# The loads of raw w_out move from the queue of SP to the queue of GpSimd

## The chip, the cores and the metric

One core of one Trainium2 chip runs the whole program. The metric is device time in microseconds (us): the median of several executions. Engines are named as in the profile: PE (TensorE), PEld (its weight load), DVE (VectorE), ACT (ScalarE), POOL (GpSimd), SP (SyncE, which here only begins transfers).

## The reference

```python
batch, n_heads, seq, head_dim = (4, 12, 448, 64)
scores = scale * np.matmul(q, k.transpose(0, 1, 3, 2))
scores = np.einsum('bhij,hg->bgij', scores, w_pre)
scores = scores - np.max(scores, axis=-1, keepdims=True)
attn = np.exp(scores)
attn = attn / (np.sum(attn, axis=-1, keepdims=True) + 1e-09)
attn = np.einsum('bhij,hg->bgij', attn, w_post)
x = np.matmul(attn, v)        # heads side by side: (1792, 768)
h = x @ w_in                  # (768, 2048)
g = h * np.clip(h + 3.0, 0.0, 6.0) / 6.0
out = g @ w_out               # (2048, 768)
```

An attention whose heads are mixed before and after the softmax, and a two-layer network on its output. w_in and w_out arrive as float64.

## The kernel before, in words

The work is cut into operations, and a planner (class `Plan`) sets the order of each engine's instructions before the program is built. Every operation names its engine, an assumed duration, what it reads and writes, and a priority. `Plan.schedule` goes forward in assumed time: each engine takes the ready operation of lowest priority number, and transfers pass through an assumed bandwidth kept per queue in `bw`. What comes out is a fixed order per engine. On the chip each engine and each queue keeps that order: an instruction that waits holds all that stand behind it.

**Attention** runs in steps s of 10 query rows (`step`, 45 per batch, R = 2 halves each in most). For 60 query rows, `scores` makes the products of queries and keys (L448), ACT copies them out of PSUM (`s`, L473), and small transfers on SP spread them by head into a tile `T_one` or `T_two` (L480, one instruction per head, 12 for each m, drawn `T_one<-s`). Then PE mixes the heads (L533), DVE takes the row maximum (`nb`, L541), ACT the exponential (`e`, L542), POOL scales the sum (`sm`, L544), DVE inverts it (`r`, L545), POOL multiplies (L551), ACT rounds to 16 bits (`eh`, L553), POOL forms the remainder (`el`, L554), PE mixes again (L570), and after some steps PE multiplies by the values (L607).

**The first layer** (`moe1`, L828) is independent work for PE that the planner puts between the steps; its results go to DRAM (`gd<-g`, L846).

**The weights.** `w_out_decode` is called 24 times, for n from 0 to 23. Each call loads 512 KB of raw float64 words (`wo<-in_w_out`, begun at L789 through `bulk`, L352 to L354, which uses SP) into one of the two places of the ring `stw`; ACT and DVE make float32 of it (L676, L679, L683, L687, L691); DVE forms sums and differences (L781); `w_store` sends the results to DRAM (`wsd<-WF`, L778). A load can begin when DVE has read the raw words of two calls earlier (L691). The decoded tiles go round in four places of `WF`, so a sum also waits for the store that still reads its place. All 24 loads fall into the attention, between 226 and 529 us.

**The second layer** (L1109) multiplies by the combinations of w_out in seven products per batch. It runs from about 560 us to the end.

Of the kernel before, what the change touches and what calls it, by code (L numbers as in the profile page):

```python
# [27 lines left out]
P = 128  # L28
# [35 lines left out]
Z_AT = 30  # L64
LAT_0, ACT_T = 1.0, 1
S_BUFS, LAT_T, LAT_B = 3, 2.0, 3.0


class Op:
# [50 lines left out]
class Plan:  # L120
# [64 lines left out]
    def schedule(self, prio, stay):  # L185

        free, wait, ready, out = {}, {}, {}, []
        bw, mode, then = {"SP": 0.0, "ACT": 0.0}, None, None
        recent = collections.deque([(0.0, 0.5, 0.5)], 60)
        for o, n in zip(self.ops, self.counts):  # L190
            o.n, o.ready, o.end = n, 0.0, None
# [22 lines left out]
        def avail(o):  # L214
            t = o.ready
            for p in {b.pool for b in o.takes}:
                x = p.ready(sum(b.pool is p for b in o.takes), self.HOP)
                if x is None:
                    return None
                t = max(t, x)  # L220
            return t

        while True:
            best = None
            for e in free:
                if e == "PE":
                    at = [(avail(x[2]), x) for x in ready[e]]
                    at = [(x, z) for x, z in at if x is not None]
                    if not at:
                        continue  # L230
                    t = max(free[e], min(at)[0])
                elif ready[e]:
                    t = free[e]
                elif wait[e]:
                    t = max(free[e], wait[e][0][0])
# [6 lines left out]
            t, e = best  # L242
            if e == "PE":
                at = [(avail(x[2]), x) for x in ready[e]]
                at = [x for z, x in at if z is not None and z <= t + 1e-9]
                x = min(at)
                x = min([z for z in at if z[2] is then] or [z for z in at if z[2].mode == mode and z[0] < x[0] + stay] or [x])
                then = x[2].then
# [15 lines left out]
            if e == "PE":  # L264
                n, fn, z = fill
# [5 lines left out]
            if e == "PE":  # L271
                o.end += self.SWITCH * (mode not in (None, o.mode))
                mode = o.mode
            free[e] = o.end
            if o.bytes:
                x, d, other = max(bw[e], t + 1.1), o.bytes / self.DMA_RATE, "ACT" if e == "SP" else "SP"
# [28 lines left out]
def body(ctx: ExitStack, tc: tile.TileContext, q4, kT, vj, wpre0, wpost0, ident0, w_in, w_out, outT):  # L305
    nc = tc.nc
    PE, ACT, DVE, POOL, SP = nc.tensor, nc.scalar, nc.vector, nc.gpsimd, nc.sync
# [14 lines left out]
    plan = Plan()  # L322
# [3 lines left out]
    def buf(pool, shape, dt, tag, name, bufs=1, ring=True):  # L326

        g = rings.setdefault((id(pool), tag), Ring(bufs)) if ring else None
        return Buf(lambda: pool.tile(shape, dt, tag=tag, name=name, bufs=bufs), g)
# [16 lines left out]
    def dma(nbytes, fn, r, w, prio, after=()):  # L346
        return plan.op("SP", 0.5, fn, r, w, prio, after, nbytes)

    def dmas(nbytes, out, src, w, prio, after=()):
        return plan.op("SP", 0.5, lambda: SP.dma_start(out(), src), [], w, prio, after, nbytes)  # L350

    def bulk(nbytes, out, src, w, prio, after=()):  # L352
        q = BULK
        return plan.op(q, 0.5 if q == "SP" else 0.4, lambda: (SP if q == "SP" else ACT).dma_start(out(), src), [], w, prio, after, nbytes, lat=LAT_B)  # L354
# [397 lines left out]
    def w_out_scale(z, n, room, prio):  # L752
        m, am1, t, p, r = (const([P, 1], F32, f"wo_{x}_{z}") for x in ("m", "am", "t", "p", "r"))
        dve(0.2, lambda: DVE.tensor_reduce(m(), wo_st()[:, :n], axis=AX.X, op=ALU.max), [(wo_st, k) for k in range(n)], [m], prio)
        top = across(m, f"wo{z}", prio + 0.1)

        def f():
            pow64(top, am1, t, p, r)
            if room > 1:
                DVE.tensor_scalar(p(), p(), float(room), None, op0=ALU.mult)  # L760
                DVE.tensor_scalar(r(), r(), 1.0 / room, None, op0=ALU.mult)

        dve(1.3, f, [top], [am1, t, p, r], prio + 0.2)
        wo_p[z], wo_r[z] = p, r
# [3 lines left out]
    def w_place():  # L768
        if not wr_ring.all:
            z = Buf(None)  # L770
            z.uses = [u for x in wf_ring.all[-3:] for u in x.uses]
            wr_ring.all += [z] * 4
        n = len(wr_ring.all)
        return Buf(lambda: WF()[:, n % 4 * 4 * P:(n % 4 + 1) * 4 * P], wr_ring)

    def w_store(name, i, t, at):
        d = ws_dram[name, i] = Buf(lambda: dram.tile([P, 4 * P], F32, name=f"wsd_{name}_{i}"))
        dma(262144, lambda: SP.dma_start(d(), t()), [t], [d], at)  # L778

    def w_sum(out, x, y, op, at):  # L780
        dve(0.69, lambda: DVE.tensor_tensor(out(), x(), y(), op=op), [x, y], [out], at, True)  # L781

    def w_out_decode(n, at, after):
        i, j = divmod(n, 4)
        m, q = divmod(i, 2)
        k = 4 * m + q + (12, 14, 0, 2)[j]
        raw = buf(rot, [P, NCC * P], I64, "stw", f"wo_{k}", 2)
        o = a_t[j] = w_place()
        bulk(524288, lambda: raw()[:, :4 * P], w_out[k // 4, k % 4], [raw], at, after)  # L789
        decode(raw, o, 4 * P, ((wo_st, k), lambda: wo_st()[:, k:k + 1]), at, (0.57, 0.66, 0.35, 0.64, 0.64))()  # L790
        if j:
            w_store((None, "P4", "P1", "P2")[j], i, o, at + 2)
        if j == 1:
            s1 = a_t["s"] = w_place()
            w_sum(s1, a_t[0], o, ALU.add, at + 2)
            w_store("P5", i, s1, at + 3)
        elif j == 2:
            w_sum(a_t[0], o, a_t[0], ALU.subtract, at + 2)
            w_store("P7", i, a_t[0], at + 3)
            w_sum(a_t["s"], a_t["s"], o, ALU.subtract, at + 2.1)  # L800
            w_store("P6", i, a_t["s"], at + 3.1)
        elif j == 3:
            w_sum(o, o, a_t["s"], ALU.subtract, at + 2)
            w_store("P3", i, o, at + 3)
        if n == 23:
            w_out_scale(0, 12, 1, at + 2)
            w_out_scale(1, 24, 4, at + 2)


    g_dram = [Buf(lambda b=b: dram.tile([P, NFC, S], F32, name=f"gd_{b}")) for b in range(B)]  # L810

    def moe1(G, fcs):
        b, gi = divmod(G, 2)
        n, t0 = GTOK[gi], 240 * gi
        x = x_sb[G]
        at = 5000 + 100 * G
        uh, u1 = uh_t[b], u1_t[b]
        if gi == 0 and b:
            dve(0.24, lambda: DVE.tensor_scalar(uh(), pw2(), u1(), None, op0=ALU.mult), [pw2, u1], [uh], -90)
        for fc in fcs:  # L820
            g, f0 = fc // HALF, fc % HALF
            ps = place(singles)
            pv = lambda ps=ps: ps()[:, :n]

            def mm(pv=pv, g=g, f0=f0):
                for cc in range(NCC):
                    for i, (w, z) in enumerate(((0, 0), (1, 0), (0, 1))):
                        PE.matmul(pv(), wi_g[g]()[:, w, f0, cc, :], x()[:, z, cc, :n],  # L828
                                  start=(cc == 0 and i == 0), stop=(cc == 5 and i == 2))

            if fc % 2 == 0:
                gt = buf(wpool, [P, 2, 240], F32, "g", f"g_{G}_{fc}", 3)
            r = lambda gt=gt, fc=fc: gt()[:, fc % 2, :n]
            if gi == 0 and b == 0:
                pool(0.25, lambda fc=fc: POOL.tensor_tensor(uh()[:, fc:fc + 1], pw2()[:, fc:fc + 1], u1(), op=ALU.mult), [(pw2, fc), u1], [(uh, fc)], -90)
            m1 = pe(0.00775 * n, mm, [x, (uh, fc), *[(wi_g[g], (k, fc)) for k in range(3)]],
               [ps, (gt, ("pe", fc % 2))], at + fc + (150 if fc >= HALF and G > 5 else 0))
            if fc % (CHAIN6 if G == 6 else CHAIN) and fc > fcs[0]:
                m0.then = m1
            m0 = m1  # L840
            act(0.44, lambda fc=fc, pv=pv, r=r: ACT.activation(r(), pv(), AF.Relu, bias=three()[:, fc:fc + 1], scale=uh()[:, fc:fc + 1]),  # L841
                [ps, (three, fc), (uh, fc)], [(gt, fc % 2)], -80)
            dve(0.37, lambda fc=fc, pv=pv, r=r: DVE.scalar_tensor_tensor(r(), r(), six()[:, fc:fc + 1], pv(),  # L843
                                                                                op0=ALU.min, op1=ALU.mult), [ps, (six, fc)], [(gt, fc % 2)], -80)
            if fc % 2:
                dma(P * 8 * n, lambda fc=fc, gt=gt: SP.dma_start(g_dram[b]()[:, fc - 1:fc + 1, t0:t0 + n], gt()[:, :, :n]), [gt],  # L846
                    [(g_dram[b], (fc // 2, gi))], 20 if G < 7 else -500)

# [42 lines left out]
    for s in range(NS + 12):  # L893
# [5 lines left out]
        while todo and todo[0][0] - 2 <= s:  # L899
            at, m, p = todo.pop(0)  # L900
# [7 lines left out]
        if s in range(W_AT, W_AT + W_BY * (NFC - HALF), W_BY):  # L908
            fc = HALF + (s - W_AT) // W_BY
# [7 lines left out]
        for C in range(16):  # L917
            b, c = divmod(C, 4)
# [99 lines left out]
    def gbuf(shape, dt, tag, name, bufs=1):  # L1018
# [6 lines left out]
                      prio=0, after=list({id(o): o for o in last_w}.values()) + [close_a])  # L1025
# [3 lines left out]
                       prio=0, after=list({id(u[1]): u[1] for u in wi_g[0].uses}.values()) + [close_a])  # L1029
# [85 lines left out]
    def out(b, m, half, o):  # L1115
        e = m
        dma(P * 4 * NH, lambda: SP.dma_start(outT[e * P:(e + 1) * P, b * S + half * NH:b * S + half * NH + NH], o()), [o], [], 20)
# [111 lines left out]
```

## Time and profile before

| | |
|---|---|
| median of 3 runs | 795.16 us (793.61 to 796.87) |
| the profiled execution, its own time | 803.97 us |
| its span | 802.2 us |
| mean granted clock of PE | 0.991 |
| PE busy | 779.3 us of the span |

The profiled execution is one of its own, about 9 us above the median of the three runs. In a profile, "busy" joins overlapping instructions; matmuls overlap, so a row like `x72` tells the pace of PE better than the duration of one. A chain of waits is followed back from the last instruction. Where an engine is idle, the profile names what ended the idle time. PEclk is the granted clock as a share of full speed.

### The profile page before, as it was taken

To read this page: it belongs to the slowest core of one execution; us is meant where nothing else is said; L and a number is where in the kernel's file an instruction comes from. 1 tells how busy PE (TensorE), PEld (TensorE's weight loads), DVE (VectorE), ACT (ScalarE), POOL (GpSimd) and SP (SyncE) were. 2 spreads that over 40 slices of the span, in tenths; PEclk is the share of its full clock that TensorE was granted. 3 is DMA by queue.
4 is the path that set the end of the run, shared out by engine and by line. 5 is a ranking of instruction groups with operands and counts; after the bars stand their busy time and mean duration, and the time that the engine had idled before them with its cause. 6 is when DMAs were issued, how large, how long until landed. Compare 5 with 4: busy or idle time off the path is not lost.

```text
span 802.2 us, 28025 instructions
## 1 busy us (share of the span) xinstructions
PE 779.3 (97%) x11616; PEld 631.3 (79%) x11616; DVE 580.3 (72%) x1152; ACT 528.1 (66%) x1044; POOL 367.7 (46%) x535
## 2 busy tenths in 40 slices
PE   6999999999999999999999989999999999999998
PEld 2566576577677768777788758768999999999998
DVE  2798886688969357778856776785678688989622
ACT  2487888698998647988775785886577465324200
POOL 2357789579988316777552665766200000000000
PEclk9999999999999999999999998999999999999999
DMA  7866653676364577665657666643699855654101
GB/s 231 228 185 188 200 173 107 217 235 206 96 188 152 160 226 250 221 187 171 206 164 255 202 199 208 188 126 119 180 287 364 292 170 175 187 170 146 41 14 52
DMA packets 100815, 147.75 MB, mean 184 GB/s; under 512 B 9840, under 2 KB 79824, under 8 KB 100688
## 3 DMA queue, kind: packets, MB, share of 16 engines
q1 hardware_dynamic: 100268, 145.31, 58.5%
q8 instruction: 91, 1.49, 0.8%
q10 hardware_dynamic: 420, 0.65, 0.3%
q14 instruction: 36, 0.29, 0.1%
HBM read 76.02 MB, written 31.20 MB: 134 GB/s over the span
## 4 chain that ended last, share of the span: by engine, by line
PE 77%; DVE 7%; DMA 5%; ACT 5%; POOL 2%; issue 2%; SPq 2%; ACTq 0%; POOLq 0%; DVEq 0%
PE single L1109 24%; PE single L828 21%; PE single L570 9%; PE single L607 8%; PE pair L448 7%; PE single L533 6%; PE single L873 3%; DVE nb L541 2%; DMA T_two<-s 2%; ACT e L542 1%; DMA wo<-in_w_out 1%; POOL e L551 1%; DMA T_one<-s 1%; ACT s L473 1%; SPq L480 1%
## 5 line engine op out<-in xcount | busy, mean ns | idle before, releaser
L828 PEld LDWEIGHTS <-wi 128*128 128x128 f16 x2304 | 213.0, 98 | 24.0 <-issue 18.3
L828 PE MATMUL single<-x,wi 128*128 128x208 f16 (+1 forms) x2304 | 228.6, 259 | 1.0 <-DVE AR L579 0.6
L554 POOL TENSOR_TENSOR el<-e,eh 128x448 f16<-128x448 f32 x156 | 166.9, 1089 | 41.5 <-ACT eh L553 39.7
L551 POOL TENSOR_SCALAR e<-e,r 128x448 f32<-128x448 f32 x180 | 129.4, 729 | 38.7 <-DVE r L545 29.4
L1109 PEld LDWEIGHTS <-ws_P 128*128 128x128 f16 x1440 | 138.0, 98 | 0.0
L542 ACT ACTIVATE e<-single,nb 128x448 f32<-128x448 f32 x180 | 113.7, 640 | 26.3 <-DVE nb L541 25.6
L541 DVE TENSOR_REDUCE nb<-single 128x1 f32<-128x448 f32 x180 | 103.5, 615 | 19.1 <-PE single L533 13.5
L841 ACT ACTIVATE g<-single,three,uh 128x240 f32<-128x240 f32 (+1 forms) x128 | 69.3, 542 | 50.9 <-PE single L828 50.3
L553 ACT ACTIVATE eh<-e 128x448 f16<-128x448 f32 x156 | 87.5, 583 | 14.3 <-POOL e L551 13.7
L448 PE MATMUL pair<-ks,qx 64*64 64x448 f32 x728 | 88.8, 552 | 4.5 <-ACT s L473 4.5
L473 ACT ACTIVATE s<-pair 128x896 f32<-128x896 f32 x90 | 82.7, 918 | 14.6 <-PE pair L448 7.8
L843 DVE SCALAR_TENSOR_TENSOR g<-g,six,single 128x240 f32<-128x240 f32 (+1 forms) x128 | 56.3, 442 | 39.9 <-ACT g L841 39.0
L570 PEld LDWEIGHTS <-eh 60*128 60x128 f16 x2496 | 66.2, 100 | 22.2 <-issue 21.0
L607 PEld LDWEIGHTS single<-AR,v 128*64 128x64 f32 (+1 forms) x1536 | 70.4, 140 | 14.2 <-issue 6.3
L607 PE MATMUL single<-AR,v 128*64 128x120 f32 (+3 forms) x1536 | 76.0, 270 | 0.7 <-ACT e L542 0.5
L570 PE MATMUL single<-wpost_h,eh 60*128 60x60 f16 x1248 | 72.2, 202 | 0.2 <-DVE x L633 0.2
L570 PE MATMUL single<-wpost_h,el 60*128 60x60 f16 x1248 | 72.2, 202 | 0.0
L570 PE MATMUL single<-wpost_l,eh 60*128 60x60 f16 x1248 | 71.9, 202 | 0.0
L1109 PE MATMUL single<-gx_P,ws_P 128*128 128x224 f16 x720 | 69.3, 259 | 0.0
L579 DVE TENSOR_SCALAR AR<-single 128x480 f32<-128x480 f32 (+1 forms) x92 | 58.2, 640 | 14.8 <-PE single L570 14.5
L581 ACT ACTIVATE AR<-single 128x480 f32<-128x480 f32 (+1 forms) x92 | 53.6, 585 | 22.5 <-PE single L570 22.0
L544 POOL TENSOR_SCALAR sm<-sm 128x2 f32<-128x2 f32 (+1 forms) x92 | 26.1, 284 | 84.3 <-ACT e L542 79.0
(240 smaller groups left out, 1161.4 us busy)
## 6 DMA issues: line engine op xcount, KB each, us to landing
T_two<-s SPq DMA_DIRECT2D x186, 105.0 KB
T_one<-s SPq DMA_DIRECT2D x144, 105.0 KB
wi<-in_w_in SPq DMA_DIRECT2D x16, 768.0 KB
wo<-in_w_out SPq DMA_DIRECT2D x24, 512.0 KB
wsd_P<-WF SPq DMA_DIRECT2D x42, 256.0 KB
wP<-wsd_P SPq DMA_DIRECT2D x36, 256.0 KB
gd<-g SPq DMA_DIRECT2D x32, 240.0 KB
gd<-g SPq DMA_DIRECT2D x32, 208.0 KB
```

Of the source, the lines that this page charges most:

```text
L448: PE.matmul(at[u]()[cc * D:cc * D + D], q()[r, o:o + D], ks_[cc]()[r, pr % 3, :], start=True, stop=True)
L473: act(0.9, lambda: ACT.activation(st(), two()[:, :, :S], AF.Copy), ps, [(st, 0), (st, 1)], at + 0.5)
L541: dve(0.53, lambda r=r: DVE.tensor_reduce(nb()[:, r:r + 1], ps[r]()[:, :S], axis=AX.X, op=ALU.max, negate=True), [ps[r]], [(nb, r)], s + 0 ...
L542: act(0.62, lambda r=r: ACT.activation(e()[:, r], ps[r]()[:, :S], AF.Exp, bias=nb()[:, r:r + 1], accum_out=sm()[:, r:r + 1]), [ps[r], (nb, ...
L551: pool(0.63, lambda r=r: POOL.tensor_scalar(e()[:, r], e()[:, r], rr()[:, r:r + 1], 1.0, op0=ALU.mult, op1=ALU.mult), [rr], [(e, r)], s + ...
L553: act(0.47, lambda r=r: ACT.activation(eh()[:, r], e()[:, r], AF.Copy), [(e, r)], [(eh, r)], s + 0.65 + 0.3 * r)
L554: pool(1.02, lambda r=r: POOL.tensor_tensor(el()[:, r], e()[:, r], eh()[:, r], op=ALU.subtract), [(e, r), (eh, r)], [(el, r)], s + 0.7 + 0 ...
L570: PE.matmul(out, x()[rows, r, js], z()[rows], start=(i == 0), stop=(i == len(mix) - 1))
L607: PE.matmul(pss[run]()[u * D:(u + 1) * D, k:k + N], v()[rows, jc, g * D:(g + 1) * D], cols(jc * H + g, rows), start=start, stop=stop)
L828: PE.matmul(pv(), wi_g[g]()[:, w, f0, cc, :], x()[:, z, cc, :n], start=(cc == 0 and i == 0), stop=(cc == 5 and i == 2))
L841: act(0.44, lambda fc=fc, pv=pv, r=r: ACT.activation(r(), pv(), AF.Relu, bias=three()[:, fc:fc + 1], scale=uh()[:, fc:fc + 1]), [ps, (thre ...
L1109: PE.matmul(ps()[:, :NH], w_view(w, y, 2 * m + i)[:, f], g(x)[:, f, :], start=(i == 0 and f == 0 and (y, x) == (0, 0)), stop=(i == 1 and f ...
```

## The change

The 24 loads become operations of POOL: `POOL.dma_start` in a queue that nothing else uses. For the planner such an operation takes 0.75 us of POOL, counts against POOL's shared port with DVE, and has a bandwidth entry of its own. Two more switches (`GD_POOL`, `WS_POOL`) are added and stand at 0: those stores stay on SP.

```diff
+GD_POOL, WS_POOL, WO_POOL = 0, 0, 1
...
-        bw, mode, then = {"SP": 0.0, "ACT": 0.0}, None, None
+        bw, mode, then = {"SP": 0.0, "ACT": 0.0, "POOL": 0.0}, None, None
...
+    def pdma(nbytes, fn, r, w, prio, after=()):
+        return plan.op("POOL", 0.75, fn, r, w, prio, after, nbytes, lat=LAT_B)
...
-        bulk(524288, lambda: raw()[:, :4 * P], w_out[k // 4, k % 4], [raw], at, after)
+        if WO_POOL:
+            pdma(524288, lambda: POOL.dma_start(raw()[:, :4 * P], w_out[k // 4, k % 4]), [], [raw], at, after)
+        else:
+            bulk(524288, lambda: raw()[:, :4 * P], w_out[k // 4, k % 4], [raw], at, after)
```

Because the planner works with other numbers, the order of all engines changes from the first of these loads on. Up to there it is the same. Each engine keeps its computing instructions, and SP loses the 24 loads (some rows below stand for several equal instructions).

SP, in the place of the trace around 460 us, before. In names, `wo_22` is raw block 22, `s_27_0` the scores of m = 27, and the last number only counts tiles.

```order
L354 DMA qx_3_2_8821<-in_q4 128x724
L778 DMA wsd_P3_3_8872<-WF_195 128x512
L354 DMA wo_22_8875<-in_w_out 128x512
L354 DMA wo_8_8926<-in_w_out 128x512
L846 DMA gd_2_7572<-g_5_2_8814 128x2x208
L480 DMA T_one_105<-s_27_0_8948 10x6x448 x4
L480 DMA T_one_105<-s_27_1_9020 10x6x448 x4
L480 DMA T_one_105<-s_27_2_9085 10x6x448 x3
```

And of the change, around the same scores:

```order
L785 DMA wsd_P5_4_8773<-WF_195 128x512
L857 DMA gd_2_7749<-g_4_14_8715 128x2x240
L484 DMA T_two_96<-s_26_2_8837 10x6x448 x4
L484 DMA T_one_105<-s_27_0_8861 10x6x448 x4
L484 DMA T_one_105<-s_27_1_8924 10x6x448 x4
L857 DMA gd_2_7749<-g_5_0_8947 128x2x208
L857 DMA gd_2_7749<-g_5_2_9013 128x2x208
```

The two loads of 512 KB that stood ahead of the score moves of m = 27 are gone from this queue.

POOL, of the change, from the load of `wo_22` to `wo_10`. `e_139` belongs to step 139.

```order
L797 DMA wo_22_8464<-in_w_out 128x512
L558 TENSOR_TENSOR el_135_8451<-e_135_8271,eh_135_8440 128x448
L548 TENSOR_SCALAR sm_137_8495<-sm_137_8495 128x2
L555 TENSOR_SCALAR e_137_8494<-e_137_8494,r_137_8524 128x448 x2
L548 TENSOR_SCALAR sm_139_8521<-sm_139_8521 128x2
L558 TENSOR_TENSOR el_137_8589<-e_137_8494,eh_137_8579 128x448 x2
L555 TENSOR_SCALAR e_139_8520<-e_139_8520,r_139_8591 128x448 x2
L558 TENSOR_TENSOR el_139_8668<-e_139_8520,eh_139_8663 128x448 x2
L797 DMA wo_8_8844<-in_w_out 128x512
L797 DMA wo_10_8867<-in_w_out 128x512
L548 TENSOR_SCALAR sm_141_8870<-sm_141_8870 128x2
```

The loads now stand between the softmax instructions of POOL, two of them next to each other ahead of step 141.

SP around 277 us, before:

```order
L778 DMA wsd_P4_0_5093<-WF_195 128x512
L778 DMA wsd_P5_0_5097<-WF_195 128x512
L778 DMA wsd_P1_0_5100<-WF_195 128x512
L778 DMA wsd_P7_0_5102<-WF_195 128x512
L354 DMA wo_2_5109<-in_w_out 128x512
L354 DMA wo_13_5111<-in_w_out 128x512
L846 DMA gd_1_5073<-g_2_2_5095 128x2x240
```

and `wo_2` in the change, on POOL:

```order
L555 TENSOR_SCALAR e_79_4522<-e_79_4522,r_79_4624 128x448 x2
L797 DMA wo_2_4650<-in_w_out 128x512
L558 TENSOR_TENSOR el_79_4707<-e_79_4522,eh_79_4643 128x448 x2
L548 TENSOR_SCALAR sm_81_4648<-sm_81_4648 128x2
L555 TENSOR_SCALAR e_81_4647<-e_81_4647,r_81_4760 128x448 x2
```

Before, `wo_2` stood behind four stores of w_out and the score moves of m = 16; now it stands in step 79, with `el_79` and all of step 81 behind it.

## Rows read from the trace of the kernel before

**Rows 1.** The page: span, busy time by engine, and the shares of the chain.
```profile
span 802.2 us, 28025 instructions
PE 779.3 (97%) x11616; PEld 631.3 (79%) x11616; DVE 580.3 (72%) x1152; ACT 528.1 (66%) x1044; POOL 367.7 (46%) x535
PE 77%; DVE 7%; DMA 5%; ACT 5%; POOL 2%; issue 2%; SPq 2%; ACTq 0%; POOLq 0%; DVEq 0%
```
**Rows 2.** Windows: length, busy time by engine, PEclk, DMA share, GB/s.
```profile
296.00:308.00 12.00, 10.39 (x136) 7.29 (x132) 6.04 (x14) 6.68 (x17) 5.24 (x10) 0.86 0.76 250
...
428.00:450.00 22.00, 20.43 (x320) 14.71 (x320) 13.46 (x29) 15.47 (x34) 8.67 (x11) 1.00 0.72 241
...
476.00:488.00 12.00, 9.09 (x114) 6.64 (x108) 7.47 (x15) 6.30 (x16) 5.94 (x8) 0.72 0.66 196
...
500.00:516.00 16.00, 15.41 (x280) 11.00 (x276) 15.23 (x29) 14.00 (x32) 12.84 (x16) 1.00 0.62 181
...
560.00:802.00 242.00, 239.08 (x2617) 237.01 (x2615) 171.86 (x264) 101.81 (x143) 6.44 (x15) 1.00 0.55 172
```
**Rows 3.** Timeline of PE: start, us, line, form, count, idle time before.
```profile
256.82 0.93 PE L533 MATMUL single<-T_two,wpre 64*64 64x448 f32 x8
257.94 3.91 PE L607 MATMUL single<-AR,v 128*64 128x120 f32 x72 [0.18 <-DVE AR L579]
...
300.87 5.58 PE L607 MATMUL single<-AR,v 128*64 128x120 f32 x72 [0.32 <-ACT e L542]
...
480.11 1.77 PE L533 MATMUL single<-T_one,wpre 64*64 64x448 f32 x8 [2.92 <-DMA T_two<-s]
481.81 5.96 PE L607 MATMUL single<-AR,v 128*64 128x120 f32 x72
```
**Rows 4.** Timeline of SP's queue, 458 to 485 us: start, us to issue.
```profile
462.04 0.93 SPq L354 DMA_DIRECT2D wo<-in_w_out  x2
463.07 0.40 SPq L846 DMA_DIRECT2D gd<-g  x1
463.59 12.85 SPq L480 DMA_DIRECT2D T_one<-s  x11
```
**Rows 5.** Instructions of lines 354 and 480: count, ns min/median/max.
```profile
L354 SPq DMA_DIRECT2D wo<-in_w_out x24: 337/445/1257, 226.8 to 528.9; - x24
...
L480 SPq DMA_DIRECT2D T_one<-s x240: 712/749/1649, 17.2 to 551.1; - x120
```
**Rows 6.** What SP's queue waited for, 226 to 560 us: total, times, longest.
```profile
SPq L480 <- DMA wo<-in_w_out: 3.7, 2, 2.8
...
SPq L354 <- DVE WF L691: 2.9, 1, 2.9
```
**Rows 7.** The chain of waits, 266 to 302 us: start, us, what.
```profile
276.93 6.95 DMA wo<-in_w_out
...
293.50 4.93 DMA wsd_P<-WF
298.45 0.69 DVE WF L781
```
**Rows 8.** Timeline of SP's queue, 426 to 451 us.
```profile
428.25 0.65 SPq L354 DMA_DIRECT2D wo<-in_w_out  x1
...
429.69 0.44 SPq L354 DMA_DIRECT2D wo<-in_w_out  x1
...
431.25 3.46 SPq L480 DMA_DIRECT2D T_two<-s  x4
```
**Rows 9.** Groups of POOL by form, 226 to 560 us: busy, mean ns, idle before.
```profile
L554 POOL TENSOR_TENSOR el<-e,eh 128x448 f16<-128x448 f32 x108 | 116.8, 1101 | 37.7 <-ACT eh L553 36.5
L551 POOL TENSOR_SCALAR e<-e,r 128x448 f32<-128x448 f32 x107 | 74.9, 711 | 24.3 <-DVE r L545 19.8 <-PE single L570 4.4
L544 POOL TENSOR_SCALAR sm<-sm 128x2 f32<-128x2 f32 x53 | 13.1, 247 | 62.9 <-ACT e L542 59.9
```
**Rows 10.** Timeline of DVE at 285 and 289 us.
```profile
285.39 1.10 DVE L683 TENSOR_SCALAR WF<-WF 128x512 int32<-128x512 int32 x1
...
288.97 0.41 DVE L683 TENSOR_SCALAR WF<-WF 128x512 int32<-128x512 int32 x1
```

More of the change, by code (lines that the diff above doesn't have):

```diff
@@ L777, in w_store @@
         d = ws_dram[name, i] = Buf(lambda: dram.tile([P, 4 * P], F32, name=f"wsd_{name}_{i}"))
-        dma(262144, lambda: SP.dma_start(d(), t()), [t], [d], at)
+        if WS_POOL:
+            pdma(262144, lambda: POOL.dma_start(d(), t()), [t], [d], at)
+        else:
+            dma(262144, lambda: SP.dma_start(d(), t()), [t], [d], at)
     def w_sum(out, x, y, op, at):
@@ L788, in w_out_decode @@
         o = a_t[j] = w_place()
-        bulk(524288, lambda: raw()[:, :4 * P], w_out[k // 4, k % 4], [raw], at, after)
+        if WO_POOL:
+            pdma(524288, lambda: POOL.dma_start(raw()[:, :4 * P], w_out[k // 4, k % 4]), [], [raw], at, after)
+        else:
+            bulk(524288, lambda: raw()[:, :4 * P], w_out[k // 4, k % 4], [raw], at, after)
         decode(raw, o, 4 * P, ((wo_st, k), lambda: wo_st()[:, k:k + 1]), at, (0.57, 0.66, 0.35, 0.64, 0.64))()
@@ L845, in moe1 @@
             if fc % 2:
-                dma(P * 8 * n, lambda fc=fc, gt=gt: SP.dma_start(g_dram[b]()[:, fc - 1:fc + 1, t0:t0 + n], gt()[:, :, :n]), [gt],
-                    [(g_dram[b], (fc // 2, gi))], 20 if G < 7 else -500)
+                by, eng = (pdma, POOL) if GD_POOL and G < 7 else (dma, SP)
+                by(P * 8 * n, lambda fc=fc, gt=gt, eng=eng: eng.dma_start(g_dram[b]()[:, fc - 1:fc + 1, t0:t0 + n], gt()[:, :, :n]), [gt],
+                   [(g_dram[b], (fc // 2, gi))], 20 if G < 7 else -500)
     for z in range(2):
```

## The prediction, made before the changed kernel ran

> **What bounds the kernel now.** First the page [rows 1]: PE is busy for 779.3 of 802.2 us and holds 77% of the chain. PE's work is the same in both kernels, so the change can move only time in which PE stands still or runs at a lower clock. Next the windows [rows 2]. From 560 us on, PE is busy for 239.08 of 242 us at full clock: nothing is to be had there. Up to the first moved load at 226.8 us [rows 5] the order does not change. What is left is the attention from 226 to 560 us. There I looked for windows in which PE falls short, and found four [rows 2]. PE is idle for 12 - 9.09 = 2.91 us in 476 to 488, for 12 - 10.39 = 1.61 in 296 to 308, for 22 - 20.43 = 1.57 in 428 to 450, and for 16 - 15.41 = 0.59 in 500 to 516.
>
> Two of these are followed by a slower PE. The mean granted clock is 0.72 and 0.86 in those windows, a mixture of full speed (2.4 GHz) and half (1.2 GHz). What that costs is read from equal work [rows 3]: 72 matmuls of L607 take 3.91 us at 258 us, but 5.96 after the idle time at 478 and 5.58 at 301; eight of L533 take 0.93 and, at 480, 1.77. So the window at 476 costs 2.91 + 2.05 + 0.84 = 5.80 us, the one at 296 costs 1.61 + 1.67 = 3.28, the others 1.57 and 0.59. Together 11.24 us: that is the most that this change can win.
>
> Then I asked what stands behind each, in the chain, SP's queue and its waits. At 476 PE waits 2.92 us for score moves [rows 3]. SP begins two loads of w_out at 462.04, then the score moves of m = 27 [rows 4]. Eleven of these take 12.85 us; at 0.749 us each [rows 5] they would take 8.24. The 4.6 us more are mostly SP waiting for the landing of w_out loads: 3.7 us in two waits [rows 6]. At 296 the chain holds a w_out load that takes 6.95 us from issue to landing and a store of a decoded tile that takes 4.93, for which DVE's sum at L781 waits [rows 7]; the row maxima of the next step stand behind that sum. At 428 two loads are issued right ahead of score moves [rows 8].
>
> **The change, part by part.** *Taken from SP:* 24 issues of 0.445 us [rows 5], 10.7 us, plus the waits for the landing of w_out (3.7 us) and for the raw ring (2.9 us) [rows 6]. What this is worth lies in the four windows.
>
> At 476: the two issues (0.93 us) and the 4.6 us go, together 5.5, more than the 2.92 that PE waited, so the idle time and the clock's fall could both go. But the bytes still move: the new order has `wo_8` and `wo_10` next to each other on POOL at about the same scores, and whatever they take from the engines the score moves lack. I take 4.0 of 5.80.
>
> At 296: `wo_2` no longer stands behind score moves and four stores, so its decoding can start earlier. But the store and the sum that waits for it remain, and in the new order too a sum stands right ahead of a row maximum. I take half, 1.6 of 3.28.
>
> At 428: two issues, 0.65 + 0.44 us, ahead of score moves [rows 8]: 1.0 of 1.57. At 500: nothing. The gain is 6.6 us; its bounds are 0 and 11.24.
>
> *Added to POOL:* 24 issues. No row shows a transfer begun by POOL. Nearest below is POOL's smallest softmax instruction, 0.247 us [rows 9]; SP takes 0.445 and at most 1.257 [rows 5]; POOL's two-input subtraction takes 1.101 [rows 9]. I take 1.1, near the upper end, because here POOL itself has to do the work of issuing. That is 26.4 us of POOL; the lower end gives 5.9, the upper 30.2. POOL has room: its three large groups are busy for 116.8 + 74.9 + 13.1 = 204.8 of 334 us and idle for 124.9 us ahead of them, waiting [rows 9]. What of it reaches PE I take from the chain: POOL holds 2% of 802.2 us, 16 us, against 204.8 us busy in the attention, about 8%. So 26.4 us cost 2.1 us, with bounds of 0.5 and 2.4. The cover is PE's first-layer work between the steps; where the planner has none, a late `el` costs its full length.
>
> *A rule against it.* The rows at L683 show DVE and POOL in each other's way: the same instruction takes 0.41 us, and 1.10 at 285 us [rows 10]. The Trainium skill (page "SBUF — State Buffer", section "SBUF: two separate sides") says that a transfer begun by GpSimd needs GpSimd to write descriptors, which it cannot do while DVE runs in a mode that holds the shared ports. No row of this trace shows that for a transfer. As a mechanism of this kernel: each decoding has one L683 of 0.41 us, so if every one of the 24 loads met one, POOL would lose 9.8 us more, of which 8% is 0.8 us. That moves the sum by less than the choice of 1.1 us does, so I leave it inside the range.
>
> *The moved order.* Every engine's order shifts after the first load. PE's work stays, so this is worth only what it opens or closes as idle time; I put it at zero, and it is the main reason why the range is wide.
>
> *Sum:* -6.6 + 2.1 = -4.5 us. Against the profiled execution's own 803.97 us (span 802.2) that is 799.5; that execution is 8.8 us above the median of the runs shown, and I carry the difference over to it: 795.16 - 4.5 = 790.7 us.
>
> **Rivals.** *A, the forecast:* the score moves come free of the loads; 790.7 us.
>
> *B, the transfer sets the pace and not the queue.* Then only issue time is saved: 0.93 us at 476, 1.09 at 428, and at 296 nothing, since the store's 4.93 us remain. 2.0 us are won and POOL takes 2.1: 795.3 us. For it speaks that at 476 and 296 the transfer engines are busy at 0.66 and 0.76 [rows 2]; against it that SP stood 3.7 us in waits for these very loads, with small moves behind them [rows 6]. The Trainium skill, page "DMA: Bandwidth & Descriptors", section "Issuing engines are not separate DMA queues", states this rule: transfers begun by several engines share the same transfer engines, and only the issue time is saved. SP's waits are what the trace shows beyond it.
>
> *C, POOL is held, and it gets slower.* A load on POOL must wait until DVE has read the raw words of two loads earlier (L691), and `sm`, `e` and `el` of the next steps stand behind it. SP had such a wait of 2.9 us [rows 6]. If POOL has one where PE has no other work, PE loses what it lost at 476: 2.91 us idle and as much again by the clock, 5.8. With one such place and half the gain the sum is -3.3 + 2.1 + 5.8 = +4.6: 799.8 us; with two, 805.6. It decides from the first wait of about 3 us that no first-layer work covers. For it: POOL is an engine of the softmax, SP is not, and DVE is itself held by stores at L781. Against it: POOL was idle for 62.9 us ahead of `sm` alone, 59.9 of it waiting for ACT [rows 9], so a short wait costs nothing, and the planner puts each load where it assumes the words are read.
>
> *D, it doesn't do what it says:* the order of the change has all 24 loads on POOL, so this has no chance worth a number.
>
> **How the numbers follow.** A 0.50, B 0.30, C 0.20. A measurement of this kernel can tell about 0.5%, 4 us, from no change: below 791.2 is faster, above 799.1 slower. A gives 0.43 faster and 0.07 the same, since it lies near the edge; B 0.03 faster, 0.26 the same, 0.01 slower; C 0.02 the same and 0.18 slower. Faster 0.46, the same 0.35, slower 0.19. The range: below, all four windows closed and POOL at its lower bound would give 795.16 - 11.24 + 0.5 = 784.4; above, C with one place, 799.8. Rounded 784.5 to 800; left out are C with two places and an order better than these windows, some 0.15. A's own range is 784.5 to 793.
>
> **What would show it.** Right: no wait of SP for w_out, eleven score moves of one m in little over 8.3 us, and fewer than four short windows from 226 to 560 us, with their idle time under 6.7 us in sum and the clock at 1.00; POOL's issues near 1.1 us, and POOL's share of the chain little above 2%. B: SP free, but PE idle in the same places, waiting for score moves in flight. C: POOL idle ahead of its transfers, ended by DVE L691, and PE or ACT waiting for `el` or `e` with a fall of the clock behind it. Wrong in kind would be a change of time ahead of 226 us or behind 560, or PE's equal work at another pace.

## The result, and the profile after

The changed kernel takes 807.71 us (median of 4 runs, 803.72 to 809.30) where the kernel before takes 794.77 beside it: a ratio of 1.0132, 95% interval 1.0099 to 1.0166. It is 1.3% slower; the forecast was 790.7, and 807.71 lies above its range. The profiled execution of before [rows 1] was 9 us above its own median, so spans of the two pages differ by only 3.1 us, and a second profile of the kernel before (span 795.4) is used beside it.

The page of the kernel after: span and busy time, the two large DMA queues (packets, MB, share), and the chain by engine, against [rows 1].

```profile
span 805.3 us, 28062 instructions
...
PE 777.9 (97%) x11616; PEld 629.4 (78%) x11616; DVE 584.9 (73%) x1152; ACT 527.7 (66%) x1044; POOL 384.2 (48%) x559
...
q1 hardware_dynamic: 96812, 132.73, 52.7%
q0 software_dynamic: 3456, 12.58, 5.5%
...
PE 65%; ACT 9%; DMA 8%; DVE 7%; SPq 4%; POOL 4%; issue 3%; ACTq 0%; POOLq 0%; DVEq 0%
```

POOL is busy for 16.5 us more, 14.4 of it for the 24 issues. The loads have a queue of their own. Against [rows 1] the chain has more of DMA, ACT, SP and POOL in it and less of PE; but the second profile of the kernel before has nearly the same shares, so they tell nothing of the change:

```profile
PE 66%; DMA 9%; DVE 9%; ACT 7%; SPq 4%; issue 3%; POOL 3%; ACTq 0%; POOLq 0%; DVEq 0%
```

Windows, columns as in [rows 2]: the attention in the profile of before, then after.

```profile
226.00:560.00 334.00, 327.14 (x5821) 253.31 (x5818) 235.47 (x485) 255.30 (x559) 207.11 (x280) 0.98 0.62 191
```
```profile
226.00:560.00 334.00, 321.18 (x5816) 248.93 (x5810) 240.31 (x496) 252.54 (x549) 222.98 (x306) 0.99 0.62 191
296.00:308.00 12.00, 11.77 (x180) 9.25 (x182) 10.58 (x20) 9.37 (x22) 11.66 (x15) 1.00 0.86 274
420.00:432.00 12.00, 7.22 (x98) 4.38 (x91) 3.39 (x6) 4.33 (x9) 3.22 (x4) 0.72 0.79 266
...
428.00:450.00 22.00, 22.00 (x364) 17.59 (x361) 15.48 (x34) 15.52 (x34) 9.06 (x15) 0.94 0.49 148
476.00:488.00 12.00, 11.69 (x210) 9.38 (x204) 9.43 (x19) 10.29 (x23) 9.81 (x13) 1.00 0.58 191
```

The three windows of the forecast's gain did close. But PE, busy for 327.14 of the 334 us from 226 to 560 in the profile of before, is now busy for 321.18: the idle time has moved elsewhere, above all to 420 to 432, where PE stands for 4.78 us and its clock falls. The second profile of before (the same columns) shows what the first hid:

```profile
226.00:560.00 334.00, 328.91 (x5882) 255.78 (x5875) 241.03 (x508) 258.66 (x564) 212.49 (x292) 1.00 0.63 194
296.00:308.00 12.00, 11.90 (x208) 8.39 (x201) 8.69 (x20) 10.84 (x26) 8.16 (x13) 1.00 0.82 262
428.00:450.00 22.00, 20.35 (x358) 14.74 (x357) 14.48 (x32) 15.76 (x35) 8.77 (x14) 1.00 0.69 225
476.00:488.00 12.00, 12.00 (x218) 10.94 (x215) 9.85 (x19) 8.85 (x22) 8.97 (x12) 1.00 0.71 216
```

Two of the three windows are full there, with the old code: what I meant to win at 296 and 476 belonged to one execution. PE is idle for 5.1 us in all from 226 to 560, at full clock.

The new stall at 420, in the timelines of POOL, SP's queue and PE of after:

```profile
419.59 0.58 POOL L797 DMA_DIRECT2D wo<-in_w_out  x1 [2.15 <-issue]
```
```profile
419.61 0.77 SPq L484 DMA_DIRECT2D T_two<-s  x1
```
```profile
426.70 1.77 PE L537 MATMUL single<-T_two,wpre 64*64 64x448 f32 x8 [4.78 <-DMA T_two<-s]
```

POOL begins half a megabyte 0.02 us ahead of a score move, which then lands after 6.89 us; PE waits 4.78 and runs on at half clock (eight of L537 take 1.77, at full clock 0.93 [rows 3]). The chain of waits goes through it, as it went through a load and a store at 296 [rows 7]:

```profile
419.61 6.89 DMA T_two<-s
426.70 1.77 PE single L537 x8
428.47 8.67 PE single L838 x72
```

The 72 matmuls of L838 behind it take 8.67 us on the chain and 8.73 in PE's timeline; the same 72 take 7.54 or 7.55 in the eleven other places of this trace. So the stall costs 4.78 + 0.84 + 1.18 = 6.8 us.

What SP's queue waits for in 226 to 560 us, the longest sums (total, times, longest), against [rows 6]:

```profile
SPq L857 <- DVE g L853: 14.6, 11, 3.4
SPq L484 <- ACT eh L557: 11.7, 16, 2.3
SPq L785 <- DVE g L853: 7.8, 6, 4.5
SPq L484 <- ACT WF L680: 7.6, 3, 6.7
```

No wait for w_out is left, as forecast. But SP waits longer for ACT and DVE, 80 us in all against 61 and 63 in the two profiles of before, so being free of the loads did not shorten its waits. POOL's 24 issues, their times (ns) and what POOL waited for ahead of them (us, times), then its subtraction from 226 to 560 us, against [rows 9]:

```profile
L797 POOL DMA_DIRECT2D wo<-in_w_out x24: 527/598/762, 219.5 to 509.4; - x24
...
  ACT e L546: 6.4, 1
  DVE WF L695: 4.2, 3
```
```profile
L558 POOL TENSOR_TENSOR el<-e,eh 128x448 f16<-128x448 f32 x108 | 118.9, 1119 | 22.1 <-ACT eh L557 21.0
```

POOL's idle time ahead of that subtraction is 22.1 us, where the two profiles of before have 37.7 and 32.6: part of what POOL took on came out of time in which it waited anyway.

### The profile page after: what moved, and what is told of

The parts are those of the page before. It is cut to its first block, busy times and chain, and to the rows that moved or that the text cites. A ratio compares the mean times of both kernels' runs of the same rounds, so it can differ in the third digit from the quotient of the medians.

```text
span 805.3 us, 28062 instructions
## 1 busy us (share of the span) xinstructions
PE 777.9 (97%) x11616; PEld 629.4 (78%) x11616; DVE 584.9 (73%) x1152; ACT 527.7 (66%) x1044; POOL 384.2 (48%) x559
## 4 chain that ended last, share of the span: by engine, by line
PE 65%; ACT 9%; DMA 8%; DVE 7%; SPq 4%; POOL 4%; issue 3%; ACTq 0%; POOLq 0%; DVEq 0%
PE single L1120 24%; PE single L838 17%; PE single L574 6%; PE pair L452 5%; PE single L611 5%; PE single L537 4%; SPq L484 4%; ACT e L546 3%; PE single L884 3%; POOL e L555 2%; DMA T_two<-s 2%; DMA wsd_P<-WF 2%; DVE nb L545 2%; DMA T_one<-s 2%; ACT eh L557 1%
## 5 line engine op out<-in xcount | busy, mean ns | idle before, releaser
L838 PEld LDWEIGHTS <-wi 128*128 128x128 f16 x2304 | 214.0, 98 | 27.0 <-issue 20.7
L838 PE MATMUL single<-x,wi 128*128 128x208 f16 (+1 forms) x2304 | 229.6, 260 | 3.4 <-ACT e L546 2.3
L558 POOL TENSOR_TENSOR el<-e,eh 128x448 f16<-128x448 f32 x156 | 169.0, 1101 | 26.6 <-ACT eh L557 24.9
L611 PEld LDWEIGHTS single<-AR,v 128*64 128x64 f32 (+1 forms) x1536 | 66.7, 136 | 14.1 <-issue 5.6
L611 PE MATMUL single<-AR,v 128*64 128x120 f32 (+3 forms) x1536 | 72.3, 263 | 1.9 <-ACT e L546 1.4
```

The source lines that it names most:

```text
L558: pool(1.02, lambda r=r: POOL.tensor_tensor(el()[:, r], e()[:, r], eh()[:, r], op=ALU.subtract), [(e, r), (eh, r)], [(el, r)], s + 0.7 + 0 ...
L611: PE.matmul(pss[run]()[u * D:(u + 1) * D, k:k + N], v()[rows, jc, g * D:(g + 1) * D], cols(jc * H + g, rows), start=start, stop=stop)
```

## The experiments

**1. The queue and the order apart.** The change does two things: the loads go through POOL, and the planner, told so, writes another order on every engine. One kernel keeps the old order of all engines and lets POOL begin the loads; one (second diff, from the changed kernel) keeps the new order and lets SP begin them.

```diff
-        bulk(524288, lambda: raw()[:, :4 * P], w_out[k // 4, k % 4], [raw], at, after)
+        plan.op("SP", 0.5, lambda: POOL.dma_start(raw()[:, :4 * P], w_out[k // 4, k % 4]), [], [raw], at, after, 524288, lat=LAT_B)
```
```diff
-            pdma(524288, lambda: POOL.dma_start(raw()[:, :4 * P], w_out[k // 4, k % 4]), [], [raw], at, after)
+            pdma(524288, lambda: SP.dma_start(raw()[:, :4 * P], w_out[k // 4, k % 4]), [], [raw], at, after)
```

Kernel before, once more: 

> The kernel before, unchanged, profiled a second time, because its first profiled execution (803.97 us) lies 9 us above the median of its runs. If the four short windows of the first profile belong to the kernel, PE is again idle for about 7 us between 226 and 560 us, in the same places. If they belonged to that one execution, an execution near 795 us has less idle time there, 2 us or less, and the forecast counted on time that is usually not lost.

Old order, POOL's queue: 

> The order of the kernel before on every engine, to the last instruction, but each load of w_out is begun by POOL at the place where the planner had it for SP. Theory 'order': the changed order made it slower and the queue is harmless, so this takes 794 us or a little less (788 to 797). Theory 'queue': the loads on POOL hold the softmax, so this takes 803 to 810 us, with POOL idle ahead of its transfers until DVE L695 of the change (L691 here) and waits for e and el behind them.

New order, SP's queue: 

> The order of the changed kernel on every engine, but each load of w_out is begun by SP at the place where the planner had it for POOL. Theory 'order': 804 to 812 us, as the changed kernel or a little above it, since SP has its 24 issues back. Theory 'queue': 792 to 797 us, as the kernel before.

Measured: the kernel before 797.24 us (one run); the old order with POOL's queue 810.27 us, ratio to before 1.018 (1.0118 to 1.0242); the new order with SP's queue 803.14 us, ratio 1.0095 (1.006 to 1.013). The second profile of before came out between its two expectations: 5.1 us idle, and of the three windows only that at 428 short again. Neither theory holds alone. The queue costs by itself, in the old order at least as much as the whole change; the order costs by itself; and the two don't add (1.8 + 0.95 against 1.32%). In the new order the queue adds 0.37%, which is within what the two intervals leave open.

In the profile of the new order with SP's queue PE is idle for 10.5 us from 226 to 560 (5.1 in the second profile of before); its three largest waits are below, the last with the score move (SP's queue) that it waits for. So its extra time is idle time of PE too; what in the order makes these waits was not tried.

```profile
226.00:560.00 334.00, 323.49 (x5814) 250.42 (x5813) 238.66 (x502) 253.61 (x554) 209.52 (x284) 1.00 0.63 193
```
```profile
288.80 1.73 PE L537 MATMUL single<-T_two,wpre 64*64 64x448 f32 x16 [2.81 <-DMA gd<-g]
```
```profile
410.75 0.98 PE L452 MATMUL pair<-ks,qx 64*64 64x448 f32 x8 [2.28 <-ACT s L477]
```
```profile
421.06 0.77 SPq L484 DMA_DIRECT2D T_two<-s  x1
```
```profile
424.39 0.98 PE L537 MATMUL single<-T_two,wpre 64*64 64x448 f32 x8 [1.71 <-DMA T_two<-s]
```

**2. Other draws of the planner.** The planner jitters its priorities by a seed, 3 in both kernels. Seeds 1 and 2, in each kernel and in the old planner's order with POOL's queue:

```diff
-DRAWS, JITTER = (3,), 0.3
+DRAWS, JITTER = (1,), 0.3
```

SP's queue: 

> The kernel before (loads begun by SP, planner as before) with another draw of the planner's jitter (seed 1 in place of 3), so another order of the work on all engines. Luck theory (the old order was a favourable draw and any other order costs the 6 to 8 us that the new order cost with SP's queue): 801 to 806 us. Systematic theory (the spread over draws is small and the cost lies in planning for and using GpSimd's queue): 793 to 800 us, as before.

 

> As the run before it with seed 2. Luck theory: 801 to 806 us. Systematic theory: 793 to 800 us.

The changed kernel: 

> The changed kernel (loads begun by GpSimd and planned so) with seed 1. Luck theory: within 3 us of the kernel before with the same seed, on either side. Systematic theory: 8 to 13 us above the kernel before with the same seed.

 

> The changed kernel with seed 2. Luck theory: within 3 us of the kernel before with seed 2, on either side. Systematic theory: 8 to 13 us above it.

The old planner's order, POOL's queue: 

> Seed 1's order of the kernel before on every engine, with the 24 loads begun by GpSimd in the places where SP began them. Queue theory (beginning a load on GpSimd costs of itself, whatever the order): 8 to 13 us above seed 1 with SP's queue (807.25), so 815 to 820 us. Tuned-order theory (only the order that the tuned seed gave is so close to the edge that a moved load hurts): within 3 us of 807.25.

 

> The same with seed 2 (806.04 us with SP's queue). Queue theory: 814 to 819 us. Tuned-order theory: within 3 us of 806.04.

Measured, ratio to the kernel before (median us):

| seed | SP's queue, old planner | its order, POOL's queue | changed kernel |
|---|---|---|---|
| 3 | 1 | 1.0180 (810.27) | 1.0132 (807.71) |
| 1 | 1.0111 (807.25) | 1.0200 (813.30) | 1.0230 (813.97) |
| 2 | 1.0099 (806.04) | 1.0113 (806.62) | 1.0115 (805.18) |

Three orders other than the old one, all with SP's queue, cost 0.95, 0.99 and 1.11%. So the order of the kernel before is a good draw, and each order tried beside it gives back about 1%. POOL's queue in one and the same order adds 1.8, 0.9 and 0.1% (each uncertain by some 0.6): it is not a fixed price, it depends on where the loads fall.

**3. A queue of ScalarE's.** The edit of 1 with `ACT.dma_start`. 

> The order of the kernel before, with the 24 loads begun by ScalarE in its own queue, in the places where SP began them. If any queue but SP's costs (the transfers begin earlier or later and collide, or SP now runs ahead): 806 to 812 us, as with GpSimd. If the cost is GpSimd's own (its time, its waits, its kind of queue): 794 to 800 us, or up to 5 us more where ScalarE itself is held by the loads' waits.

Measured: 839.06 us, ratio 1.0525. Neither expectation was met: with two such queues SP's own issues come to wait for the loads of the other, for 86.3 us in the four sums below (what SP's queue waited for, 226 to 600 us). So this run says nothing of POOL.

```profile
SPq L480 <- DMA wo<-in_w_out: 30.6, 7, 8.0
SPq L778 <- DMA wo<-in_w_out: 21.0, 6, 5.5
SPq L846 <- DMA wo<-in_w_out: 18.0, 6, 5.4
SPq L354 <- DMA wo<-in_w_out: 16.7, 3, 11.9
```

**4. POOL's time, without and with a DMA.** Loads begun by SP in the old order; beside each, POOL does two memsets of a small tile of its own, six of them, or begins a load of one column into such a tile (second diff).

```diff
-        bulk(524288, lambda: raw()[:, :4 * P], w_out[k // 4, k % 4], [raw], at, after)
+        plan.op("SP", 0.5, lambda: (SP.dma_start(raw()[:, :4 * P], w_out[k // 4, k % 4]), POOL.memset(idle(), 0.0), POOL.memset(idle(), 0.0)), [], [raw], at, after, 524288, lat=LAT_B)
```
```diff
+        plan.op("SP", 0.5, lambda: (SP.dma_start(raw()[:, :4 * P], w_out[k // 4, k % 4]), POOL.dma_start(idle[n % 4](), w_out[k // 4, k % 4][:, :1])), [], [raw], at, after, 524288, lat=LAT_B)
```

Two memsets: 

> The kernel before, loads begun by SP as before, and on GpSimd, in each of the 24 places, two memsets of a tile of 128x1 that nobody reads (about 0.25 us each, so some 0.5 us, close to the 0.6 us that beginning a load took there; 12 us in all). If GpSimd's time is what costs: 803 to 810 us. If it is the queue, the waits or the landing of the loads: 794 to 800 us.

Tiny loads: 

> The kernel before, its 24 loads begun by SP, and beside each of them GpSimd begins a load of one column of the same block (128x1, 1 KB in place of 512 KB) into a tile that nobody reads, in the place where it began the whole load in the old order with GpSimd's queue. Issue theory (what costs is the time in which GpSimd begins a load, about 0.6 us each, during which and behind which VectorE's two-input operations are held): 802 to 810 us, with some of VectorE's operations over 1 us beyond their least time at those places. Transfer theory (what costs is that half a megabyte now moves beside the score moves of SP's queue, where it used to stand in line with them): 794 to 801 us.

Six memsets: 

> As x_pool_idle, but six memsets of 128x1 in each of the 24 places (0.098 us each there, so 0.59 us a place, the time that beginning a load takes; two were only 0.2). If GpSimd's delay of 0.6 us is enough for its next operations to come in front of VectorE's sum at the place of the load at 511: 803 to 806 us and that sum at about 5 us, as with the tiny loads. If it is the beginning of a DMA itself that does it: 797 to 800 us and the sum under 2 us.

Measured: 799.29 us, ratio 1.0011 (0.9976 to 1.0047); 804.76, 1.0107 (1.0058 to 1.0157); 798.34, 1.0011 (0.998 to 1.0042). Two memsets took only 0.2 us a place, hence the third kernel. So 0.6 us of POOL's time in each place shows no cost (the interval leaves up to 0.4%); beginning a DMA does cost, even with almost no bytes. The largest place is one sum of VectorE, at 505 us: with the tiny loads the last `e` starts 8.3 us later than in the second profile of before, and 4.5 of that come in behind this sum. DVE and POOL with the tiny loads:

```profile
505.65 5.45 DVE L781 TENSOR_TENSOR WF<-WF 128x512 f32<-128x512 f32 x1
```
```profile
504.69 0.58 POOL L789 DMA_DIRECT2D idle<-in_w_out  x1
505.32 1.25 POOL L551 TENSOR_SCALAR e<-e,r 128x448 f32<-128x448 f32 x2
506.55 4.00 POOL L554 TENSOR_TENSOR el<-e,eh 128x448 f16<-128x448 f32 x4
```

and with six memsets:

```profile
504.98 1.07 DVE L781 TENSOR_TENSOR WF<-WF 128x512 f32<-128x512 f32 x1
```
```profile
504.03 0.88 POOL L789 MEMSET idle<- 128x1 f32 x6
504.87 1.68 POOL L551 TENSOR_SCALAR e<-e,r 128x448 f32<-128x448 f32 x2
506.53 4.02 POOL L554 TENSOR_TENSOR el<-e,eh 128x448 f16<-128x448 f32 x4
```

Behind the memsets the sum slips in beside POOL's `e` (which takes 1.68 in place of 1.25) and ends after 1.07 us. Behind the begun load it stands until the six instructions that follow the load on POOL are through, at 510.55, and ends 0.55 later. The same sum takes 4.99 us with the whole loads of experiment 1, and ACT's `e` behind it waits 4.36 us for the row maxima:

```profile
512.76 4.99 DVE L781 TENSOR_TENSOR WF<-WF 128x512 f32<-128x512 f32 x1 [0.37 <-DMA wsd_P<-WF]
```
```profile
518.88 0.63 ACT L542 ACTIVATE e<-single,nb 128x448 f32<-128x448 f32 x1 [4.36 <-DVE nb L541]
```

The Trainium skill, page "SBUF — State Buffer", section "SBUF: two separate sides", has a lock on a pair of ports that VectorE and GpSimd share, held for a whole instruction. That agrees with DVE's wait; that the wait can last through six instructions of POOL is what these runs add.

How general is it? In the traces from 220 to 570 us I counted DVE instructions, of those that don't read PSUM, over 1 us longer than the least of their form. The eight traces (of seven kernels) in which POOL begins no DMA have none. The eleven in which it does have 19 that begin and end in this stretch (after: 3; nine of the eleven have one or more). They are not sums alone: L683, which reads one tile, takes 4.82 us in one place (seed 2, old planner's order with POOL's queue) where its least is 0.41.

The instant at which the DVE instruction begins does not explain it by itself. In the eight traces 782 such instructions begin while POOL is at work with its next instruction less than 0.1 us behind, and none of them lets more than one further instruction of POOL go first. In the eleven, 14 let two to five go first. All 14 begin 0.1 to 4.2 us after POOL has begun a DMA; 183 others that begin within 4.2 us of one do not wait so long, and of the 957 that begin at other times none does. So in these traces a begun DMA is a condition of the long wait, and not enough for it; what else it takes, the runs don't tell.

**5. Four loads of 24.** In the old order with POOL's queue, PE falls behind at two places above all. The n-th `e` of one trace answers to the n-th of the other, since the orders are the same: from the second profile of before to this one, the lag grows by 4.2 us at the 293rd (which starts at 463.88 there, at 470.31 here) and by 4.5 at the 323rd, the one behind the sum above. At the first place the trace has (POOL, SP's queue, PE; the matmuls read T_two, though the release is put down to another transfer):

```profile
456.56 1.13 POOL L789 DMA_DIRECT2D wo<-in_w_out  x2
```
```profile
457.39 0.77 SPq L480 DMA_DIRECT2D T_two<-s  x1
```
```profile
466.17 1.77 PE L533 MATMUL single<-T_two,wpre 64*64 64x448 f32 x8 [3.21 <-DMA T_one<-s]
```

In the kernel before, the same two loads stand behind that score move in SP's queue. From the move's issue to PE's use of it there: 461.26 - 456.09 = 5.2 us; here 466.17 - 457.39 = 8.8.

```profile
456.09 0.77 SPq L480 DMA_DIRECT2D T_two<-s  x1
...
458.60 0.95 SPq L354 DMA_DIRECT2D wo<-in_w_out  x2
```
```profile
461.26 0.98 PE L533 MATMUL single<-T_two,wpre 64*64 64x448 f32 x8 [0.52 <-DMA wsd_P<-WF]
```

So these four loads (two at each place) were given back to SP, and then given alone to POOL; and seven loads that SP begins in the three windows of the forecast or just behind them (from 299 to 320, 428 to 430 and 487 to 491 us in the first profile of before) were given to POOL alone. These seven are not the loads on which the forecast built most of its gain: 4.0 us of it stood on the two at 462 us, which are the first place of the four, and 1.6 on `wo_2` at 277. Only the two at 428, with 1.0 us, are its own.

```diff
+        plan.op("SP", 0.5, lambda: (SP if n in (17, 18, 21, 22) else POOL).dma_start(raw()[:, :4 * P], w_out[k // 4, k % 4]), [], [raw], at, after, 524288, lat=LAT_B)
```

Four given back: 

> The old order with the loads on GpSimd (810.27 us), but the four loads that stood at 456.6 (two), 509.7 and 511.4 us in that trace are given back to SP. Place theory (the 13 us are a few stalls: a score move that lands 3 to 5 us late beside the two loads at 456.6, and a sum of VectorE that took 4.99 us behind the load at 511.4): 799 to 803 us. Diffuse theory (each load costs its share, 13/24 us): 807 to 810 us.

Four alone: 

> The reverse: the kernel before with those four loads alone on GpSimd, 20 on SP. Place theory: 803 to 807 us. Diffuse theory: 797 to 800 us.

Seven in or behind the windows: 

> The order of the kernel before with GpSimd beginning only the seven loads (6th to 8th, 16th, 17th, 20th, 21st) that stand in SP's queue in the three windows from which the prediction took its gain. By the prediction's sum: 6.6 us less than before less 0.6 for GpSimd, so 789 to 792 us. By the place theory (the windows' idle time was mostly not SP's doing, and these loads meet neither of the two stalls): 794 to 800 us.

Measured: 799.89 us, ratio 1.0046 (1.0018 to 1.0075); 806.79, 1.0134 (1.009 to 1.0178); 800.59, 1.0026 (0.9992 to 1.0059). Of the 1.8% of 24 loads, four make 1.3 and twenty make 0.5 (each uncertain by 0.3 to 0.6). The four alone show both stalls again, the 293rd `e` later by 4.6 us, the sum 5.11 us. With the tiny loads, which move 1 KB each, the first place costs only 1.6 us and the second 4.5: the first is mostly bytes, the second is the issue.

The forecast's gain does not show at any of its places in the old order. The two loads at 462 cost 4.6 us on POOL. Those at 428, together with the five others, bring nothing (1.0026). And `wo_2`, which with all 24 loads on POOL begins 7 us earlier than in the second profile of before (268.40 against 275.52 us), leaves every `e` from the 157th to the 237th (240 to 368 us) within 0.6 us of where it was; it was not moved alone.

**6. One load in the changed kernel.** The load at 419.59 us given back to SP, in the new order.

```diff
-            pdma(524288, lambda: POOL.dma_start(raw()[:, :4 * P], w_out[k // 4, k % 4]), [], [raw], at, after)
+            pdma(524288, lambda: (SP if n == 16 else POOL).dma_start(raw()[:, :4 * P], w_out[k // 4, k % 4]), [], [raw], at, after)
```

> The changed kernel with one load of 24 given back to SP, the one that GpSimd began at 419.59 us, 0.02 us ahead of the score move at 419.61 that landed only after 6.89 us. Transfer theory: TensorE's wait for that move falls from 4.8 to about 1.7 us (as in the new order with SP's queue) and the time by about 3 us, to 803 to 806 us. If the move is late for another reason: 806 to 809 us.

Measured: 804.95 us, ratio 1.0096 (1.0063 to 1.0128), as much as the new order with all loads on SP (1.0095). PE's wait at that move is 3.01 us in place of 4.78, with the clock kept (eight of L537 in 0.98), not the 1.7 expected from the new order with SP's queue:

```profile
424.13 0.98 PE L537 MATMUL single<-T_two,wpre 64*64 64x448 f32 x8 [3.01 <-DMA T_two<-s]
```

The time fell as the transfer theory said, the wait by some 60% of what it said. The difference of the two ratios, 0.36%, is not larger than what each interval leaves open; the wait and the clock are the firmer evidence.

No version tried beats the kernel before.

## Why the prediction was wrong

Three steps failed: the idle windows of one execution were taken for the kernel's, the moved order was put at zero, and the price of the new queue was taken to be POOL's time.

**What bounds the kernel.** Held: outside the attention the changed kernel runs as before (the 130th `e` starts at 204.74 us, in the second profile of before at 205.95; from the last `e` to the end it takes 241.63 us, before 242.35). What it loses is idle time and clock in the attention. But "together 11.24 us" was read from one execution that was 8.8 us above the median, and carried over to the median as if its stalls were the kernel's. The second profile has no idle time to speak of at 476 and 296 and no fall of the clock. Its span is 6.8 us shorter. Less idle time (5.1 against 6.9 us) and the 4.6 us that the prediction put to the clock make 6.3 of these: the stalls were what made that execution long.

**At 476, at 296, at 428 (6.6 us).** The mechanism was half right: SP's waits for w_out went, as did the idle time in these windows. But 4.0 and 1.6 of the 6.6 had only been there in the one execution; and in the old order POOL's queue brings nothing at 428 or behind `wo_2`, and costs 4.6 us at the two loads of 462.

**Added to POOL (2.1 us).** The issue takes 0.598 us, not 1.1, so 14.4 us, not 26.4. 8% of 14.4 us would be 1.2 us or 0.14%; the six memsets, with 0.6 us in each place, cost nothing measurable (1.0011, up to 1.0042), which is too coarse to tell this share from none. The larger price lay in what the term did not contain: VectorE held behind a begun load, 4.5 us in one place of the old order. In the changed kernel such holds are shorter, 1.0 to 1.5 us beyond the least in three places.

**A rule against it.** I had POOL waiting for DVE and priced that at 0.8 us of POOL. The runs show the other direction: DVE waits for POOL, and in the old order DVE's sum stands ahead of a row maximum, on the path. This was the right pair of engines with the wrong one held.

**The moved order.** "I put it at zero", without a reason: this failed. The new order with SP's queue costs 0.95%, some 7.6 us, of the 1.32%. Taken the other way round, the queue alone costs 1.8% in the old order, so the runs do not rank this step against the queue's. The order before was the best of four; an edit that makes the planner draw anew can lose that, whatever the edit is. The trace of before could not show it. The new order was known before the run, but only a run of another draw could have put a price on it.

**Rival B** was nearest in its rule and wrong in its sign: that the bytes still move was right, but the term has no zero for an end. In SP's queue a load stood behind score moves; in its own it can begin ahead of one (0.02 us at 419.59, 0.83 at 456.56). From the move's issue to PE's use of it then take 7.1 and 8.8 us, where the same order with SP's queue has 3.3 and 5.2. The Trainium skill, page "DMA: Bandwidth & Descriptors", section "Issuing engines are not separate DMA queues", says that transfers of several issuers share the engines and interleave: the rows agree. With the one load at 419.59 given back, PE's wait of 4.78 us fell by 1.8 (one profile of each), so that load is a part of it; what makes the rest was not found.

**Rival C** came near in time with two places (805.6), but by luck: its mechanism is not what was found. POOL did wait for L695, three times and 4.2 us in all; the longest of these waits, 3.04 us at 329 us, has no idle time of PE over 0.3 us behind it until 355.

## What to carry to other kernels

Where a planner or a scheduler sees the edit, try the edit in the old order, and the new order without the edit: here the two cost 1.8 and 0.95%, and did not add up to the 1.32 of both. A queue is also an order: a bulk load that stood behind small urgent transfers can begin ahead of them when it gets a queue of its own. And a gain read from windows of one execution is worth nothing until a second execution shows the same windows.

## What was unexpected in the hardware

Beginning a load on POOL takes 0.53 to 0.77 us for 512 KB and 0.53 to 0.77 for 1 KB: it doesn't go by the bytes, and its median of 0.598 is longer than SP's 0.445 [rows 5]. A VectorE sum of 0.67 us took 4.99, 5.11 and 5.45 us in three kernels in which POOL began a DMA at that place, and 0.91 to 1.57 us in the seven other traces of that order, without one there. With no DMA begun on POOL, DVE let at most one further instruction of POOL go first, in all of the 782 cases counted above.
